# Attention with a gated unit on one core: a third bank shared by two engines, gates read from PSUM, and two small operations of the head moved

## The chip, the cores and the metric

The kernel runs on one core of a Trainium2 chip. The core has TensorE (PE; its weight loads are listed as PEld), VectorE (DVE), ScalarE (ACT), GpSimd (POOL) and SyncE (SP, which issues DMAs). The metric is the device time of one execution in microseconds; lower is better. Times of runs are given as medians, and one further execution was recorded by the hardware profiler.

## The reference

The input is 2048 rows of 640 numbers. Attention with 32 heads of 20 runs on the normalised rows, a gated unit with 1728 hidden columns runs on the same rows, and the two results are multiplied and added to the input:

```
xn = _layernorm(x, axis=-1)
q, k, v = split((xn @ wqkv), 32 heads of 20)
s = softmax(q k^T / sqrt(20)) v, heads joined, @ wo
h = sigmoid(xn @ w_gate) * (xn @ w_up)
g = silu(h @ w_down)
out = x + s * g
```

## The kernel before

**Head.** x is loaded in tiles of 128 rows. For each tile VectorE (two of the tiles: ScalarE) gathers mean and variance, ScalarE takes the root, VectorE inverts it and multiplies it with the negative mean (`ln_scale`, rstd L240, nb L241), GpSimd applies both (`ln_apply`, L245), TensorE transposes the tile (L254) and ScalarE copies it into xnT (L257). The first four heads of k are computed there; their largest absolute values (mk, L135 and L132) make a bound on the scores (`bound`, L318, ScalarE), TensorE adds it to q (L283), and ScalarE writes qT (L288). Behind its tiles GpSimd fills several buffers, the largest of them wo_pad (L357).

**Main part.** There are 32 passes, one for each quarter of the rows (512 queries) and each group of four heads. A pass has 64 banks: 16 tiles of 128 keys times four heads, each a score matmul of 512 columns into one PSUM bank (`score`, L1140). Most banks get their exp on ScalarE (`act_exp`, L1162): two sets of PSUM banks, sc0 with three and sc1 with two, are filled in turn, and one ACTIVATE does a whole set. Some banks get theirs on VectorE (`dve_exp`), in four instructions over 512 columns (dy L1173, du L1178, du L1182, p L1186); their scores go to a bank called spare, which is one of two banks (misc0, misc1) that all other matmuls use too. The probabilities are multiplied with v into a bank called oacc (`pv`, L1274), whose 21 rows for each head hold the sum of probabilities beside the result. When a pass is done, oacc is copied (L771), and the sums go through DRAM, are inverted and come back (L772 to L800).

**Between the exps** stand jobs that use TensorE's free time: gate and up products (L643, L656, with a tanh on ScalarE, L650, and a product on VectorE, L660), down products (`down_job`, L679: two halves of 320 columns, each copied to d2 by VectorE, L683; a tanh over 640 columns on ScalarE, L690; then a gate on VectorE, L695), output products (L718), and, for the last quarter, part products without the last two groups (`part_job`, L750, L755) to which GpSimd adds x by DMA (L758).

**The order is written out by a planner.** While the program is built, Python code keeps a clock for TensorE and a queue with durations and due times for ScalarE and VectorE, and emits the instructions in the order in which this plan starts them. Each engine then works its own list off in that order; what one needs of another is a semaphore wait. The planner lets TensorE multiply zeros into a free bank (`zero_add`, L1250) when fewer than 2.5 us of the last 3.4 us were counted as streaming. A cell (`Cell`) holds the planned time at which a bank or a value is free.

**The end.** The last pass is done in two halves of 256 queries. The first half's result is inverted in a job (`half_job`), the second half's behind the main loop (from L1369): copy of oacc, sums picked by a matmul (L1383), reciprocal (L1388), spread (L1390) and transposed by a matmul (L1392), scaled (L1394), multiplied with wo for the last two groups (L1376), gated (`gated`, L871), added up and sent out (`summed`, L874, L875).

Of the kernel before, what the change touches and what calls it, by code (L numbers as in the profile page):

```python
# [15 lines left out]
P = 128  # L16
HEAD = 32
GH = 4
# [26 lines left out]
def kernel(  # L45
# [116 lines left out]
    with tc.tile_pool(name="setup", bufs=1) as sp, \  # L162
# [76 lines left out]
        def ln_scale(t0, n):  # L239
            nc.vector.reciprocal(out=rstd[:, t0:t0 + n], in_=rstd[:, t0:t0 + n])  # L240
            nc.vector.scalar_tensor_tensor(out=nb[:, t0:t0 + n], in0=mv[:, t0:t0 + n, 0], scalar=-1.0,  # L241
                                           in1=rstd[:, t0:t0 + n], op0=ALU.mult, op1=ALU.mult)
# [68 lines left out]
        for c in range(4):  # L311
# [5 lines left out]
        op(("kbound",), "ACT", 0.3, [("kmost",)],  # L317
           lambda: nc.scalar.activation(out=bound, in_=esum, func=ACT.Identity, scale=mk[:, DENSE:DENSE + 1]))  # L318
# [56 lines left out]
    class Cell:  # L375
        def __init__(self, t=None):
            self.t = t

# [287 lines left out]
    def down_job(tt):  # L666
        c, t4 = divmod(tt, QC // P)
        yield "known", lambda: (bulk[0] == NFT and pe[0] > bulk_t[0] + LANDED and len(h_cells.get(c, [])) == NFT and (tt < 2 or tt - 2 in gq_cells)
                                and (c < NQC - 1 or front() >= PER_PASS * (NG * c + t4 + 1)))
        yield "wait", h_cells[c] + ([gq_cells[tt - 2]] if tt > 1 else [])  # L670
        hT = hTs[c]
        d2 = glu[0].tile([P, D], FP32, tag="d2", bufs=2, name="d2")
        got = []
        for h in range(2):
            e0_, e1_ = h * HALF, (h + 1) * HALF
            held, psd = yield "bank",
            for kf in range(NFT):
                fsz = fsz_list[kf]
                nc.tensor.matmul(psd[:, 0:HALF], lhsT=hT[0:fsz, kf, t4 * P:(t4 + 1) * P],  # L679
                                 rhs=glu[1][0:fsz, kf, e0_:e1_], start=(kf == 0), stop=(kf == NFT - 1))  # L680
                yield "mm", MM3
            got.append(dve.add(400.0, [Cell(pe[0] + PE_OUT)], lambda psd=psd, e0_=e0_, e1_=e1_:
                               nc.vector.tensor_copy(out=d2[:, e0_:e1_], in_=psd[:, 0:HALF]), 1))  # L683
            give_bank(held, got[-1])
        d_cells.setdefault(c, []).append(Cell(pe[0]))
        made = {}

        def tanh():
            made["t"] = glu[0].tile([P, D], BF16, tag="td", bufs=1, name="td")
            nc.scalar.activation(out=made["t"], in_=d2, func=ACT.Tanh, scale=0.25)  # L690

        def finish():
            last = c == NQC - 1
            gq = kT_all[:, t4, :].bitcast(FP32)[:, 0:D] if last else d2
            nc.vector.scalar_tensor_tensor(out=gq, in0=made["t"], scalar=1.0, in1=d2, op0=ALU.add, op1=ALU.mult)  # L695
            if last:
                gq_last[t4] = gq
            else:
                nc.gpsimd.dma_start(out=gq_dram[tt, :, :], in_=d2)

        turned = act.add(590.0, got + td_free[-1:], tanh, 0, EXP_LAG)
        td_free.append(dve.add(740.0, [turned], finish, 2))
        gq_cells[tt] = td_free[-1]
# [102 lines left out]
    half = {}  # L806

    def first_half(done):
        def copy():
            half["oev"] = glu[0].tile([P, KD, P], BF16, tag="wg", bufs=WB, name="oev")  # L810
            half["oev"] = half["oev"].rearrange("p k f -> p (k f)").bitcast(FP32)[:, 0:QH]
            nc.vector.tensor_copy(out=half["oev"], in_=oacc[:, 0:QH])

        cell = dve.add(340.0, [Cell(done + PE_OUT)], copy, -1)
        half["cell"] = cell
        return cell

    def half_job():
        n, tiles = QH // P, range(QH // P)
        yield "wait", [half["cell"]]  # L820
        held, pd = yield "bank",
        for t4 in tiles:
            nc.tensor.matmul(pd[:, t4 * GH:(t4 + 1) * GH], lhsT=half["oev"][:, t4 * P:(t4 + 1) * P], rhs=pick,
                             start=True, stop=True, skip_group_check=True)
            yield "mm", MM3
# [6 lines left out]
        def spread():  # L832
            made["rb"] = glu[0].tile([P, KD, P], BF16, tag="wu", bufs=WB, name="rb")
            made["rb"] = made["rb"].rearrange("p k f -> p (k f)").bitcast(FP32)[:, 0:n * P].rearrange(
                "p (t j i) -> p t j i", t=n, j=GH)
            nc.vector.tensor_copy(out=made["rb"], in_=made["rq"].unsqueeze(3).to_broadcast([P, n, GH, 32]))
# [6 lines left out]
        for t4 in tiles:  # L843
            nc.tensor.matmul(prl[:, t4 * P:(t4 + 1) * P], lhsT=made["rb"][:, t4, :, :].rearrange("p j i -> p (j i)"),
                             rhs=identf, start=True, stop=True, skip_group_check=True)
            yield "mm", 2 * MM5

        def scale():
            oTs[steps[-1]] = wk.tile([P, QC], BF16, tag="oT", bufs=NG + 3, name="oT")
            nc.vector.tensor_tensor(out=oTs[steps[-1]][:, 0:QH], in0=half["oev"], in1=prl[:, 0:QH], op=ALU.mult)  # L850

        cell = dve.add(340.0, [Cell(pe[0] + PE_OUT)], scale, -1)
# [4 lines left out]
        for t4 in tiles:  # L857
            got = []
            for h in range(2):
                held, ps = yield "bank",  # L860
                for g in range(NG - 2, NG):
                    nc.tensor.matmul(ps[:, 0:HALF], lhsT=oTs[NQC - 1, g][:, t4 * P:(t4 + 1) * P],
                                     rhs=wo_pad[:, g, h * HALF:(h + 1) * HALF], start=(g == NG - 2), stop=(g == NG - 1))
                    yield "mm", MM3
                got.append(dve.add(400.0, [Cell(pe[0] + PE_OUT)], lambda t4=t4, h=h, ps=ps: gated(t4, h, ps), 1))
                give_bank(held, got[-1])
            dve.add(740.0, [out_cells[(NQC - 1) * 4 + t4], *got], lambda t4=t4: summed(t4, pair[:, t4 % 2 * D:(t4 % 2 + 1) * D]), 2)
# [12 lines left out]
    LAST, QH = NB - PER_PASS, QC // 2  # L880
# [6 lines left out]
    HALF_COST = 12 * MM3 + 4 * MM5  # L887
# [46 lines left out]
    for t4 in range(4):  # L934
        jobs.append(Job(part_job(t4), PART_COST, len(steps) - 1, NB - (40 if t4 < 2 else 16)))
    jobs.append(Job(half_job(), HALF_COST, len(steps) - 1, NB - 12, when=lambda: half))
# [83 lines left out]
    def runnable(p):  # L1020
        k = 0
        while True:
            if k == len(flight):
                if k == MOST:
                    return None
# [12 lines left out]
    def fill(p, room=1e18):  # L1038
# [4 lines left out]
        pe_do("fill", took)  # L1043
# [24 lines left out]
    NEEDED, NEEDED_LAST = 6, 12  # L1068
# [36 lines left out]
    def dve_bank(banks):  # L1105
# [3 lines left out]
        ends = LAST + PER_PASS // 2 if LAST <= b < LAST + PER_PASS // 2 else PER_PASS * (b // PER_PASS + 1)  # L1109
# [12 lines left out]
    def unit(b):  # L1122
        return b // PER_PASS if b < LAST else len(steps) - 1 + (b - LAST) // (PER_PASS // 2)

    def pieces(b):
        r = b % PER_PASS
        if b < LAST:
            return [(r // GH, 0, 0, QC)]
        half, r = divmod(r, PER_PASS // 2)
        return [(2 * (r // GH) + k, half * QH, k * QH, QH) for k in range(2)]  # L1130

    def full(p):
        return KT if p < len(steps) - 1 else KT // 2
# [62 lines left out]
    def issue():  # L1196
# [6 lines left out]
        if (ci > 1 and dve.backlog + max(0.0, dve.t - pe[0]) < D_BACKLOG  # L1203
                and all(c.t is not None for c in d_made[-2:-1])):
            extra = dve_bank(taken)
            if extra is not None:
                split = take_bank("spare")
        ps = psum.tile([P, n, 512], FP32, tag=f"sc{ci % 2}", bufs=1, name="sc")
# [3 lines left out]
        sets[ci % 2] = act_exp(ps, taken, begun)  # L1212
# [10 lines left out]
    def pv_batch():  # L1223

        p = pv_pass[0]
        if p > len(steps):
            return None
# [36 lines left out]
    def pv(batch):  # L1264
# [3 lines left out]
        for k in range(2):  # L1268
            for part in range(1 if p < len(steps) - 1 else 2):
# [18 lines left out]
        if all(n == most for n in pv_count[0]):  # L1288
# [4 lines left out]
            elif p == len(steps) - 1:  # L1293
                oacc_free[0] = first_half(pe[0])
# [10 lines left out]
    while pv_pass[0] <= len(steps):  # L1305
# [47 lines left out]
        if zero_add(room):  # L1353
            idle = False
            continue
        soon = [q[k][1].made.t for q in ready_p for k in range(min(2, len(q)))]
        times = [until, pe[0] + 150.0] + [t + SEM for t in soon if t is not None]
        pe[0] = min(t for t in times if t > pe[0] + 1.0)

    while flight or jobs or timed or act.queue or dve.queue:  # L1360
# [5 lines left out]
    tiles = range(QH // P, QC // P)  # L1366
    units = [(t4, h) for t4 in tiles for h in range(2)]
    oev = wk.tile([P, QC], FP32, tag="oev", bufs=OBUFS, name="oev")
    nc.vector.tensor_copy(out=oev[:, QH:], in_=oacc[:, QH:])  # L1369
# [3 lines left out]
    banks, pd, prl = banks[1:5], banks[6], banks[7]  # L1373
# [6 lines left out]
    for bank, (t4, h) in zip(banks[:3], units):  # L1380
        out_mm(bank, t4, h, NG - 2)
    for k, t4 in enumerate(tiles):
        nc.tensor.matmul(pd[:, k * GH:(k + 1) * GH], lhsT=oev[:, t4 * P:(t4 + 1) * P], rhs=pick,  # L1383
                         start=True, stop=True, skip_group_check=True)
    out_mm(banks[3], *units[3], NG - 2)
# [5 lines left out]
    for k, t4 in enumerate(tiles):  # L1391
        nc.tensor.matmul(prl[:, t4 * P:(t4 + 1) * P], lhsT=rb[:, k, :, :].rearrange("p j i -> p (j i)"), rhs=identf,  # L1392
                         start=True, stop=True, skip_group_check=True)
    nc.vector.tensor_tensor(out=oTs[qc, g][:, QH:], in0=oev[:, QH:], in1=prl[:, QH:], op=ALU.mult)  # L1394
# [34 lines left out]
```

## Time and profile before

| | us |
|---|---|
| median of 3 runs | 894.62 (894.53 to 898.45) |
| the profiled execution | 898.68 |
| its span | 896.5 |
| ScalarE busy in the span | 871.4 (97%) |
| VectorE busy | 838.6 (94%) |
| TensorE busy | 809.1 (90%) |
| GpSimd busy | 161.6 (18%) |
| granted TensorE clock, mean | 0.99 |

The span is the time from the first to the last instruction of the profiled execution. An engine's busy time counts overlapping instructions once; the time of one instruction is longer than what it adds, because the next one starts before it has ended. Idle time is put down to whatever released the instruction behind it.

### The profile page before, as it was taken

Reading aid. Unit: us, or ns where it says so; the run is one execution under the profiler, and the core shown is the slowest. Engines: PE = TensorE matmul, PEld = TensorE weight load, DVE = VectorE, ACT = ScalarE, POOL = GpSimd, SP = SyncE. Lnnn points to the kernel's source line nnn. Section 1 sums busy time; section 2 is a strip of 40 time slices with the busy share of each in tenths; the row PEclk is TensorE's granted clock in tenths of the full one; section 3 lists DMA queues with packets and bytes.
Section 4 is the critical chain, followed back from the end, with each engine's and each line's share of the span. In section 5 each row is a group of like instructions: output and inputs, shape, how many; then the busy total and the mean of one; then the engine's idle time right before and its main releaser. Section 6 shows DMA issues by size and latency. Waiting matters only on the chain.

```text
span 896.5 us, 16915 instructions
## 1 busy us (share of the span) xinstructions
PE 809.1 (90%) x6228; PEld 291.8 (33%) x6311; DVE 838.6 (94%) x1483; ACT 871.4 (97%) x837; POOL 161.6 (18%) x305
## 2 busy tenths in 40 slices
PE   5899899998998999999999998999999888999896
PEld 3344333332223333232233332222332322333342
DVE  7799999999999999997999999999999989999994
ACT  6999999999999999999999999999999999999993
POOL 7401111101111212111111221110121220111120
PEclk9999999999999999999999999999999999999996
DMA  8113231235442234223212342303022432200021
GB/s 316 46 36 89 68 105 35 56 94 150 120 122 41 64 89 71 64 58 79 56 25 79 95 65 65 78 24 79 27 73 64 107 64 67 56 20 14 14 59 45
DMA packets 107672, 64.40 MB, mean 72 GB/s; under 512 B 80350, under 2 KB 101906, under 8 KB 107498
## 3 DMA queue, kind: packets, MB, share of 16 engines
q1 hardware_dynamic: 97382, 47.21, 19.8%
q0 software_dynamic: 10208, 16.11, 8.0%
q8 instruction: 49, 0.80, 0.4%
q14 instruction: 33, 0.27, 0.1%
HBM read 50.45 MB, written 16.13 MB: 74 GB/s over the span
## 4 chain that ended last, share of the span: by engine, by line
ACT 63%; issue 18%; PE 11%; DVE 7%; DMA 1%; SPq 0%; ACTq 0%; DVEq 0%
ACT p L1162 58%; PE sc L1140 4%; ACT tnh L650 3%; PE oacc L1274 2%; DVE dy L1173 1%; PE work L643 1%; PE work L123 1%; DVE du L1178 1%; PE work L679 1%; ACT td L690 1%; DVE stats L226 1%; DVE p L1186 1%; DVE du L1182 1%; PE work L149 1%; DMA x_sb<-in_A_x_dram 0%
## 5 line engine op out<-in xcount | busy, mean ns | idle before, releaser
L1162 ACT ACTIVATE p<-sc 128x1536 bf16<-128x1536 f32 x717 | 828.9, 1361 | 3.4 <-PE oacc L1274 1.4
L1140 PE MATMUL sc<-qT,kT_all 21*128 21x512 bf16 (+1 forms) x1850 | 280.9, 377 | 56.5 <-ACT p L1162 48.5
L1173 DVE TENSOR_SCALAR dy<-spare 128x512 f32<-128x512 f32 x256 | 175.2, 685 | 22.6 <-PE spare L1140 20.0
L1140 PEld LDWEIGHTS <-kT_all 21*128 21x128 bf16 x2112 | 90.9, 91 | 286.8 <-issue 275.1
L1182 DVE SCALAR_TENSOR_TENSOR du<-du,dy 128x512 f32<-128x512 f32 x256 | 174.1, 683 | 1.6
L1186 DVE SCALAR_TENSOR_TENSOR p<-du,dy 128x512 uint16<-128x512 f32 x256 | 174.0, 682 | 1.3
L1178 DVE SCALAR_TENSOR_TENSOR du<-dy 128x512 f32<-128x512 uint16 x256 | 174.2, 684 | 0.8
L1274 PE MATMUL oacc<-p,v_all 128*21 128x512 bf16 (+1 forms) x2112 | 158.3, 379 | 0.6 <-DVE v_all L156 0.3
L1140 PE MATMUL spare<-qT,kT_all 21*128 21x512 bf16 (+1 forms) x262 | 98.2, 379 | 0.0
L772 POOL DMA_DIRECT2D den_dram<-oev x31 | 17.9, 578 | 392.8 <-DVE oev L771 392.8
L679 PE MATMUL work<-wd,hT 128*128 128x320 bf16 x448 | 85.5, 302 | 0.1
L643 PE MATMUL work<-xnT,wg 128*128 128x512 bf16 (+1 forms) x261 | 77.6, 383 | 2.0 <-issue 0.6
L656 PE MATMUL work<-xnT,wu 128*128 128x512 bf16 (+1 forms) x268 | 73.1, 381 | 1.2 <-DVE dy L1173 0.3
L788 POOL DMA_DIRECT2D rl<-rec_dram x124 | 61.5, 502 | 57.6 <-DMA rec_dram<-den 47.8
L1250 PE MATMUL oacc<-xnT,zero 128*128 128x512 bf16 x169 | 57.9, 391 | 3.7 <-issue 2.9
L1274 PEld LDWEIGHTS <-v_all 128*21 128x21 bf16 x2112 | 31.4, 90 | 62.9 <-issue 60.7
L679 PEld LDWEIGHTS <-hT 128*128 128x128 bf16 x448 | 35.0, 97 | 48.7 <-issue 39.1
L650 ACT ACTIVATE tnh<-work 128x512 bf16<-128x512 f32 (+1 forms) x56 | 41.4, 738 | 0.0
L660 DVE SCALAR_TENSOR_TENSOR hT<-tnh,work 128x512 bf16<-128x512 bf16 (+1 forms) x56 | 38.0, 679 | 2.2 <-ACT tnh L650 1.9
L782 POOL DMA_DIRECT2D rec_dram<-den x31 | 16.9, 546 | 119.9 <-DVE den L781 115.4
L718 PE MATMUL work<-wo_pad,oT 128*128 128x320 bf16 x192 | 35.5, 302 | 0.5 <-issue 0.5
L643 PEld LDWEIGHTS <-wg 128*128 128x128 bf16 (+1 forms) x280 | 21.7, 98 | 42.8 <-issue 31.1
(122 smaller groups left out, 554.9 us busy)
## 6 DMA issues: line engine op xcount, KB each, us to landing
wg<-in_B_w_gate_dram SPq DMA_DIRECT2D x52, 160.0 KB
wu<-in_B_w_up_dram SPq DMA_DIRECT2D x52, 160.0 KB
rl<-rec_dram POOLq DMA_DIRECT2D x124, 64.0 KB, 2.4
qT<-q_dram SPq DMA_DIRECT2D x31, 128.0 KB
gq_dram<-d POOLq DMA_DIRECT2D x12, 320.0 KB, 2.5
gqr<-gq_dram SPq DMA_DIRECT2D x12, 320.0 KB
kT_all<-k_dram SPq DMA_DIRECT2D x28, 128.0 KB
wd<-in_B_w_down_dram SPq DMA_DIRECT2D x13, 160.0 KB
```

The costliest lines, as they stand in the source:

```text
L643: nc.tensor.matmul(psg[0:fsz, :], lhsT=wg[:, kd, 0:fsz], rhs=xnT[:, kd, cols], start=(kd == 0), stop=(kd == KD - 1))
L650: nc.scalar.activation(out=made["t"][0:fsz, :], in_=psg[0:fsz, :], func=ACT.Tanh, scale=0.5)
L656: nc.tensor.matmul(psu[0:fsz, :], lhsT=wu[:, kd, 0:fsz], rhs=xnT[:, kd, cols], start=(kd == 0), stop=(kd == KD - 1))
L679: nc.tensor.matmul(psd[:, 0:HALF], lhsT=hT[0:fsz, kf, t4 * P:(t4 + 1) * P], rhs=glu[1][0:fsz, kf, e0_:e1_], start=(kf == 0), stop=(kf == N ...
L788: nc.gpsimd.dma_start(out=t["rl"][32 * j:32 * j + 32, :], in_=rec_dram[n, j:j + 1, :].to_broadcast([32, QC]))
L1140: nc.tensor.matmul(ps[:, c0:c0 + n], lhsT=kT_all[rows, g, kt * P:(kt + 1) * P], rhs=qTs[qc, g][rows, q0:q0 + n], start=True, stop=True, ti ...
L1162: nc.scalar.activation(out=buf.tile(), in_=ps, func=ACT.Exp, bias=EXP_BIAS, scale=exp_scale)
L1173: nc.vector.tensor_scalar(out=t["y"], in0=ps, scalar1=LEAST, scalar2=None, op0=ALU.max)
L1178: nc.vector.scalar_tensor_tensor(out=t["u"], in0=t["f"], scalar=CUBE_2, in1=t["f"], op0=ALU.add, op1=ALU.mult)
L1182: nc.vector.scalar_tensor_tensor(out=t["u"], in0=t["u"], scalar=CUBE_1, in1=t["f"], op0=ALU.add, op1=ALU.mult)
L1186: nc.vector.scalar_tensor_tensor(out=buf.tile()[:, 0, :].bitcast(U16), in0=t["u"], scalar=CUBE_SCALE, in1=t["y"], op0=ALU.mult, op1=ALU.add)
L1274: nc.tensor.matmul(oacc[32 * j:32 * j + 1 + Dh, q0:q0 + width], lhsT=v_all[:, kt, GH * g + j, 0:1 + Dh], rhs=buf.ap[:, i, c0:c0 + width], ...
```

## The change

Four things are changed.

1. In the head, nb is made tile by tile with a `tensor_scalar`, rstd being a scalar operand, in place of one two-tensor operation for each batch; the first bound is made by VectorE in place of ScalarE.
2. A set of three banks may be shared: ScalarE gets two of them and VectorE the third, when no own bank is at hand and VectorE's planned backlog is under 1.3 us.
3. The halves of the down product are no longer copied: ScalarE's tanh and VectorE's gate read them in PSUM, 320 columns at a time.
4. The last pass is described by a list of parts (still 256 and 256 queries). Its jobs have other due times and other counted costs, are put first among the jobs in flight when their part is ready, and use other buffers. Zero matmuls stop ahead of the next planned probability, the sum of the first part's last tile is made behind the main loop, and four zero matmuls stand in the end.

The core of the diff:

```diff
+PARTS = ((0, 256), (256, 256))
...
-            nc.vector.scalar_tensor_tensor(out=nb[:, t0:t0 + n], in0=mv[:, t0:t0 + n, 0], scalar=-1.0,
-                                           in1=rstd[:, t0:t0 + n], op0=ALU.mult, op1=ALU.mult)
+            for t in range(t0, t0 + n):
+                nc.vector.tensor_scalar(out=nb[:, t:t + 1], in0=mv[:, t, 0:1], scalar1=rstd[:, t:t + 1], scalar2=-1.0,
+                                        op0=ALU.mult, op1=ALU.mult)
...
-        op(("kbound",), "ACT", 0.3, [("kmost",)],
-           lambda: nc.scalar.activation(out=bound, in_=esum, func=ACT.Identity, scale=mk[:, DENSE:DENSE + 1]))
+        op(("kbound",), "DVE", 0.15, [("kmost",)],
+           lambda: nc.vector.tensor_scalar(out=bound, in0=esum, scalar1=mk[:, DENSE:DENSE + 1], scalar2=None, op0=ALU.mult))
...
+        def tanh(h, psd):
+            made[h] = glu[0].tile([P, HALF], BF16, tag="td", bufs=2, name="td")
+            nc.scalar.activation(out=made[h], in_=psd[:, 0:HALF], func=ACT.Tanh, scale=0.25)
+        def gate(h, psd):
...
+            nc.vector.scalar_tensor_tensor(out=made["gq"][:, h * HALF:(h + 1) * HALF], in0=made[h], scalar=1.0,
+                                           in1=psd[:, 0:HALF], op0=ALU.add, op1=ALU.mult)
...
-            got.append(dve.add(400.0, [Cell(pe[0] + PE_OUT)], lambda psd=psd, e0_=e0_, e1_=e1_:
-                               nc.vector.tensor_copy(out=d2[:, e0_:e1_], in_=psd[:, 0:HALF]), 1))
-            give_bank(held, got[-1])
+            turned = act.add(320.0, [Cell(pe[0] + PE_OUT + 100.0), *td_free[-2:-1]], lambda h=h, psd=psd: tanh(h, psd), 0, EXP_LAG)
+            td_free.append(dve.add(400.0, [turned], lambda h=h, psd=psd: gate(h, psd), 1))
+            give_bank(held, td_free[-1])
...
-            yield "mm", MM3
+            yield "mm", 250.0, 0.0
...
-            yield "mm", 2 * MM5
+            yield "mm", 330.0, 200.0
...
+            end = lambda t4=t4: summed(t4, pair[:, t4 % 2 * D:(t4 % 2 + 1) * D])
+            if u == len(PARTS) - 2 and t4 == tiles[-1]:
+                later.append(end)
+            else:
+                dve.add(740.0, [out_cells[(NQC - 1) * 4 + t4], *got], end, 2)
...
+        shared = None
+        if (not split and n == 3 and ci > 1 and dve.backlog + max(0.0, dve.t - pe[0]) < SHARE
+                and all(c.t is not None for c in d_made[-2:-1]) and dve_bank(taken[:2]) == taken[2]):
+            shared = taken.pop()
         ps = psum.tile([P, n, 512], FP32, tag=f"sc{ci % 2}", bufs=1, name="sc")
         for i, b in enumerate(taken):
             score(ps[:, i, :], b)
             issued(b)
-        sets[ci % 2] = act_exp(ps, taken, begun)
+        sets[ci % 2] = act_exp(ps[:, 0:len(taken), :] if shared is not None else ps, taken, begun)
+        if shared is not None:
+            score(ps[:, 2, :], shared)
+            issued(shared)
+            sets[ci % 2] = Both(sets[ci % 2], dve_exp(ps[:, 2, :], shared, begun))
...
+        due = min([t for t in soon if t is not None], default=pe[0]) if b0 >= NB else 1e18
+        if zero_add(min(room, due - pe[0] - MM5)):
...
+    take_part(len(PARTS) - 1, pe[0])
     while flight or jobs or timed or act.queue or dve.queue:
...
-    for bank, (t4, h) in zip(banks[:3], units):
+    def keep_clock(n):
+        for _ in range(n):
+            nc.tensor.matmul(unused, lhsT=zero, rhs=xnT[:, 0, 0:512], start=True, stop=True, skip_group_check=True)
...
+    for end in later:
+        end()
...
+    keep_clock(2)
```

`Both` is a cell that is free when each of its two cells is. `first_half` and `half_job` are renamed to `take_part` and `last_job`, and take the part's number.

## The prediction

> **What bounds the kernel now.** I read four views in this order: the page's busy shares and chain, busy time by stretch, groups by form, and the timelines of head and end.
>
> ```profile
> PE 809.1 (90%) x6228; PEld 291.8 (33%) x6311; DVE 838.6 (94%) x1483; ACT 871.4 (97%) x837; POOL 161.6 (18%) x305
> ...
> ACT 63%; issue 18%; PE 11%; DVE 7%; DMA 1%; SPq 0%; ACTq 0%; DVEq 0%
> ```
>
> ScalarE is the fullest engine and carries most of the chain; VectorE is close behind. Busy time by stretch (columns: stretch, length, then PE, PEld, DVE, ACT, POOL busy; then TensorE clock):
>
> ```profile
> 60.00:860.00 800.00, 737.26 (x5585) 256.17 (x5662) 764.67 (x1312) 798.77 (x746) 128.47 (x236) 1.00 0.27 67
> 870.00:876.00 6.00, 5.63 (x76) 3.12 (x64) 5.32 (x13) 6.00 (x6) 2.93 (x5) 1.00 0.44 101
> 876.00:883.80 7.80, 7.47 (x66) 2.70 (x63) 3.98 (x7) 6.34 (x6) 0.00 (x0) 0.50 0.30 84
> 883.80:896.50 12.70, 5.35 (x36) 2.50 (x34) 4.68 (x10) 0.00 (x0) 0.00 (x0) 0.63 0.07 26
> ```
>
> Over 800 us ScalarE stands for 1.2 us, so there a us of ScalarE work, or of ScalarE waiting, is a us of kernel. At 876 the granted clock halves, and ScalarE loses time to TensorE for the first time. The last exp ends at 883.7; 12.8 us follow without ScalarE.
>
> The span is 896.53 us and this execution took 898.68, so 2.15 lie outside. The plain runs gave 894.53, 894.62 and 898.45. The profiled one is of the longer kind; the half-clock end (about 1.8 us of ScalarE gaps after 876, some 2 us more behind) is as large as that difference, so I read 894.6 as the same kernel with its clock kept. The sum goes against 898.68.
>
> **ScalarE's work.** From the timeline, start to start where the next instruction follows at once, medians: exp on 1536 columns 1330 ns, on 1024 columns 903.5, tanh on 512 (L650) 476.5, tanh on 640 from SBUF (L690) 627. The built order of the changed program has 341, 379 and 1 exps of three, two and one bank, where before had 358, 359 and 0: ten banks go to VectorE (266 for 256). The gain is 17 x 1.330 - 20 x 0.9035 - 0.48 = **4.1 us**. The sixteen 640-wide tanhs become 32 on 320 columns from PSUM. No such row exists. The PSUM rows lie on a line (50 ns + 0.833 ns a column), which gives 0.317; bounds are half the 640 row (0.31) and the whole 512 row (0.48). I take the line: 32 x 0.317 - 16 x 0.627 = **+0.1** (0 to +5). Four of the old tanhs started late, by 0.54, 0.48, 0.11 and 0.47 us, two of them behind this:
>
> ```profile
> L690 ACT ACTIVATE td<-d 128x640 bf16<-128x640 f32 x16 | 13.0, 812 | 0.6 <-ACT p L1162 0.3 <-DVE d L683 0.2
> L683 DVE COPY d<-work 128x320 f32<-128x320 f32 x32 | 15.3, 479 | 0.0
> ```
>
> The copies go; TensorE is late next. I take **-1.0** of 1.6 (0 to -1.6).
>
> VectorE loses 32 copies (0.40 each, start to start) and 16 gates of 640 (0.735), and gains 32 gates of 320 (0.40, as L724) and ten four-step exps (4 x 0.60): +12 us, inside the 35 us it idles between 60 and 860. That costs nothing while the cover lasts; without it, ScalarE would wait for late probabilities. Gating from PSUM holds a bank until both tanh and gate are done, which is why own-bank exps on VectorE fall from 256 to 247 in the built order, and 19 use the third bank of a shared set.
>
> **The shared sets add a wait.** The third bank is a slice of the tile that ScalarE reads, and the built order shows that two readers of one tile are put one behind the other:
>
> ```
> Activation p2_3803<-sc_3785 128x1024 [waits DVE_49,Activation_49]
> TensorScalarPtr dy_3071<-sc_3055 128x512 [waits Activation_49]
> ```
>
> In before no exp waits for VectorE and no dy for ScalarE. Now ten exps wait for dy on the same set (case A), and nine dys for the exp (case B).
>
> A: scores end a median 0.29 us ahead of their exp in the trace; dy starts 0.07 or more behind its score and takes 0.68 (L1173); a semaphore takes about 0.07. ScalarE, its queue blocked, waits 0.07 + 0.68 + 0.07 - 0.29 = 0.53: ten make 5.3. Between the tenth and the eightieth percentile of that lead (0.10 to 0.58) it is 0.24 to 0.72.
>
> B: an exp of two banks lasts 1.14 from start to end; then 0.07, dy 0.68, 0.07, and the next scores 0.40: 2.36 after the exp began the set is full again. ScalarE has the other set until 1.81. It waits 0.55, less where a tanh (0.48) stands between; 0.45 x 9 = 4.1. From below 0 (a tanh each time), from above 0.9. Behind the waiting dy stand the other exps and gates of VectorE, which its idle time takes up. Together **+9.4** (2 to 15).
>
> **The head.** nb becomes a TENSOR_SCALAR for each tile (16 for 12), and the first bound moves from ScalarE (L318, 0.39 us) to VectorE. Timelines of POOL, DVE and ACT:
>
> ```profile
> 20.71 2.59 POOL L245 TENSOR_SCALAR x_sb<-x_sb,rstd,nb 128x640 bf16<-128x640 bf16 x3 [0.52 <-DVE nb L241]
> 27.99 4.69 POOL L357 MEMSET wo_pad<- 128x5120 bf16 x1
> ```
>
> ```profile
> 20.95 0.64 DVE L241 SCALAR_TENSOR_TENSOR nb<-mv,rstd 128x1 f32<-128x1 f32 x1
> ...
> 28.40 0.16 DVE L132 TENSOR_REDUCE mk<-mk_all 128x1 f32<-128x4 f32 x1
> ```
>
> ```profile
> 28.90 0.39 ACT L318 ACTIVATE bound<-esum,mk 128x128 bf16<-128x128 bf16 x1
> 29.77 0.69 ACT L288 ACTIVATE qT<-ps_q,e_one 128x512 bf16<-128x512 f32 x1 [0.48 <-PE ps_q L283]
> ```
>
> The nb at 20.95 takes 0.64 where others take 0.16: it ends at 21.59, as the first of POOL's three instructions ends (20.71 + 0.86). So a VectorE instruction can wait out a whole POOL instruction; another lost 0.43 at 8.93. The reduction at 28.40 ran at its usual 0.16 beside a POOL memset, so not each one does. Which kind is the new bound? It reads and writes 16-bit data in SBUF, like L568, which does 512 columns in 0.29 us where other forms take 0.68: it uses more access to SBUF than a plain stream, as the two-input nb does. So L241 is the row it is nearest to. It would be ready at 28.56, in the middle of the 4.69 us memset, and wait until 32.68. From bound's start to the first exp before took 30.99 - 28.90 = 2.1; less 0.2 for the shorter instruction, the exp starts at 34.6: **+3.6**. If it does not wait, bound ends near 28.8, qT follows the two kT_all at about 29.3, and the head gains 0.5. nb by itself: two stalls of 0.45 gone at best, 16 at 0.14 (L522) for 12 at 0.11 at worst (+0.9); taken as 0. POOL's order is unchanged.
>
> The Trainium skill, page "SBUF — State Buffer", section "Who interferes with whom", says that a copy, cast or tensor_scalar in a mode using two ports, and a GpSimd instruction, exclude each other for the whole instruction of whichever starts first. It speaks against this edit; the stalls of L241 agree, while no row here shows a TENSOR_SCALAR of VectorE beside a POOL memset. By it the first exp is at 34.6, without it at 30.5.
>
> **The end.** The rest of the last pass is counted by what it streams, with filler matmuls only up to the next probability, so I expect the clock to hold: -1.8 us of ScalarE gaps. Before, the last PV batch waited behind six zero matmuls at half clock and ended at 886.23, 2.5 us behind the last exp; now 0.45. But the built order puts work behind it that had been done earlier: one part product, the gating and sum of tile 1, and VectorE's sum of tile 0. Two gates 0.8, the part product 0.85 and its gate 0.4, the sum 0.74 and the waits between set the reciprocal about 4.0 behind the last exp, as before (4.05). The stretch behind it (8.7) stays. End: **-2.0** (-4 to +1).
>
> **Sum.** -4.1 + 0.1 - 1.0 + 9.4 + 3.6 - 2.0 = +6.0: 898.7 + 6.0 = **904.7**, 10 above the median shown.
>
> **Rivals.**
> - Bound isn't held (the reduction at 28.40 speaks for it): 904.7 - 4.1 = 900.6.
> - Not slower: the waits of shared sets are covered, because dy runs ahead of need. It decides on dy ending before ScalarE is through the other set, so a lead of 0.82 us or more, against the median 0.29. Sum without 9.4, and no hold: 898.7 - 7.5 = 891.2; with the hold 895.3.
> - Worse: with TensorE idle for 4 us in the head its clock drops as at 876, and dys stand behind other work: 4 more, 908 to 909.
> - Not doing what it says: the clock halves in the end all the same: +2 to +4 on any of these.
>
> Chances: forecast 0.5, not held 0.27, covered 0.15, worse 0.08. The range 896 to 909 holds the first two with their bounds and some of the others. A measurement can tell about 0.5% here (890.1 to 899.1 is no change): faster 0.05, same 0.19, slower 0.76.
>
> **What would show it.** An exp p2<-sc waiting for DVE dy, about ten times 0.5 us; ScalarE gaps after dy on sc; ACT exp busy 4 us less; bound on VectorE lasting 4 us, ending with wo_pad's memset, first exp near 34.6; clock 1.00 past 876; reciprocal some 4 us behind the last exp. I am wrong if ScalarE's idle time between 60 and 860 stays at 1 to 2 us, or bound takes 0.2.

## The result, and the profile after

The changed kernel takes **916.37 us** (913.97 to 918.28, 4 runs), the kernel before 896.46 us beside it: a ratio of 1.0229, 95% interval 1.0205 to 1.0252. The four runs of before are two near 894.6 and two near 898.4. The forecast was 904.7, the range ended at 909: the direction held, the size did not. The profiled execution of the changed kernel took 918.11 (span 916.2), 19.4 more than the profiled one of before.

Busy shares, chain and the exps' group on the page after:

```profile
PE 812.6 (89%) x6212; PEld 292.5 (32%) x6294; DVE 855.3 (93%) x1512; ACT 871.2 (95%) x856; POOL 161.6 (18%) x305
...
ACT 50%; PE 17%; issue 16%; DVE 15%; POOL 1%; DMA 1%; SPq 0%; DVEq 0%; ACTq 0%; POOLq 0%
...
L1185 ACT ACTIVATE p<-sc 128x1536 bf16<-128x1536 f32 (+2 forms) x721 | 829.1, 1319 | 17.3 <-PE sc L1163 9.4
```

ScalarE is busy as long as before (871.2 to 871.4) in a span 19.7 longer, though its exps are fewer: where nothing follows at once, an instruction counts with its full length (1.58 us for an exp of 1536 columns, against 1.33 from start to start). VectorE's share of the chain has doubled from 7 to 15%: it now stands between exps. Three places hold the time: from the span's start to the first exp 35.57 us (30.99 before), from there to the end of the last exp 865.0 (852.7; below, this is the stretch of exps), behind it 15.6 (12.8).

**The head.** Timelines of POOL, DVE, ACT and PE, after:

```profile
28.05 4.69 POOL L359 MEMSET wo_pad<- 128x5120 bf16 x1
...
28.51 4.42 DVE L320 TENSOR_SCALAR bound<-esum,mk 128x128 bf16<-128x128 bf16 x1
...
33.40 1.54 PE L150 MATMUL ps_v<-wv,xnT 128*128 128x160 bf16 x10 [5.22 <-DVE v_all L157]
...
33.70 0.69 ACT L290 ACTIVATE qT<-ps_q,e_one 128x512 bf16<-128x512 f32 x1 [4.28 <-remote]
```

Bound starts 0.46 us after the memset and ends at 32.93, 0.19 after it. qT waits for it, and TensorE is idle for 5 us; its clock halves at 30.72, 2.5 us after its last matmul ended (28.17).

**The shared sets.** Waits after (columns: total, times, longest); none of the three is in the trace of before:

```profile
DVE dy L1196 <- ACT p L1185: 9.5, 9, 1.4
...
PE sc L1163 <- DVE dy L1196: 7.3, 9, 1.3
...
ACT p L1185 <- DVE dy L1196: 4.3, 8, 1.6
```

One set of each kind in the timeline. First dy behind its exp, then an exp behind its dy:

```profile
215.54 0.69 DVE L1196 TENSOR_SCALAR dy<-sc 128x512 f32<-128x512 f32 x1 [1.18 <-ACT p L1185]
...
216.29 0.39 PE L1163 MATMUL sc<-qT,kT_all 21*128 21x512 bf16 x3 [1.20 <-DVE dy L1196]
...
216.72 1.45 ACT L1185 ACTIVATE p<-sc 128x1536 bf16<-128x1536 f32 x1 [0.30 <-PE spare L1163]
...
267.96 0.68 DVE L1196 TENSOR_SCALAR dy<-sc 128x512 f32<-128x512 f32 x1
...
268.74 3.28 ACT L1185 ACTIVATE p<-sc 128x1024 bf16<-128x1024 f32 x3 [0.50 <-DVE dy L1196]
```

From dy's start to ScalarE's next start it takes 1.18 us in the first case (0.69 of dy, the hand-over, the scores) and 0.78 in the second (dy and the hand-over).

**The clock.** Busy time by stretch (columns as in the prediction):

```profile
30.72:37.55 6.83, 4.15 (x19) 2.27 (x20) 3.36 (x6) 2.14 (x2) 2.87 (x8) 0.50 0.08 16
37.55:218.46 180.91, 167.45 (x1307) 63.96 (x1319) 175.40 (x317) 177.98 (x158) 22.21 (x42) 1.00 0.27 74
218.46:221.87 3.41, 3.08 (x15) 0.51 (x14) 3.41 (x7) 2.96 (x3) 0.00 (x0) 0.50 0.07 14
...
269.66:279.90 10.24, 9.87 (x35) 2.29 (x35) 6.50 (x11) 6.96 (x8) 0.00 (x0) 0.50 0.21 49
279.90:727.04 447.14, 405.89 (x3081) 141.97 (x3122) 427.18 (x730) 443.00 (x431) 76.91 (x140) 1.00 0.27 64
727.04:730.45 3.41, 3.41 (x20) 1.01 (x17) 3.41 (x7) 1.93 (x2) 1.08 (x2) 0.50 0.47 79
```

TensorE's granted clock halves three times in the middle (and in the head from 30.72 to 37.55). In the middle TensorE is then the full engine, and from 269.66 on ScalarE works 6.96 of 10.24 us. Past 876, where the profile before fell to half, the clock is 1.00 up to 911.36.

**The end.** Timeline after, then the instructions of the closing line (columns: shortest, median, longest in ns; first and last start) of after and of before:

```profile
904.35 0.87 POOL L767 DMA_DIRECT2D hT<-in_A_x_dram  x1 [7.90 <-DVE hT L764]
...
905.10 0.21 DVE L1428 RECIPROCAL rq<-last 128x8 f32<-128x8 f32 x1 [0.32 <-PE last L1420]
...
909.85 0.83 DVE L890 TENSOR_TENSOR ot<-kT_all,hT 128x640 bf16<-128x640 f32 x1
```
```profile
L1465 POOLq DRAIN  x3: 51/93/11086, 904.3 to 915.9; - x3
L1465 SPq DRAIN  x3: 7/7/7, 913.0 to 915.7; - x3
```
```profile
L1424 POOLq DRAIN  x3: 51/102/11127, 874.3 to 896.2; - x3
L1424 SPq DRAIN  x3: 7/7/7, 895.7 to 896.0; - x3
```

POOL's closing drain lasts 11.1 us in both, from its last DMA on. Before, it was over at 885.4. After, that DMA (x added to the last tile's part product) is issued at 904.35, behind the last exp, and the drain ends at 915.4: SyncE, done at 913.0, waits for it.

### The profile page after: what moved, and what is told of

The parts are those of the page before. It is cut to its first block, busy times and chain, and to the rows that moved or that the text cites. A ratio compares the mean times of both kernels' runs of the same rounds, so it can differ in the third digit from the quotient of the medians.

```text
span 916.2 us, 16861 instructions
## 1 busy us (share of the span) xinstructions
PE 812.6 (89%) x6212; PEld 292.5 (32%) x6294; DVE 855.3 (93%) x1512; ACT 871.2 (95%) x856; POOL 161.6 (18%) x305
## 3 DMA queue, kind: packets, MB, share of 16 engines
q1 hardware_dynamic: 97382, 47.21, 19.4%
## 4 chain that ended last, share of the span: by engine, by line
ACT 50%; PE 17%; issue 16%; DVE 15%; POOL 1%; DMA 1%; SPq 0%; DVEq 0%; ACTq 0%; POOLq 0%
ACT p L1185 46%; PE sc L1163 5%; DVE dy L1196 4%; DVE du L1201 3%; PE oacc L1305 2%; DVE du L1205 2%; PE work L666 2%; PE work L653 2%; DVE p L1209 2%; ACT tnh L660 2%; PE work L705 1%; PE work L124 1%; ACT td L687 1%; DVE stats L227 1%; PE work L586 1%
## 5 line engine op out<-in xcount | busy, mean ns | idle before, releaser
L1185 ACT ACTIVATE p<-sc 128x1536 bf16<-128x1536 f32 (+2 forms) x721 | 829.1, 1319 | 17.3 <-PE sc L1163 9.4
L1205 DVE SCALAR_TENSOR_TENSOR du<-du,dy 128x512 f32<-128x512 f32 x266 | 180.3, 682 | 1.9
L1196 DVE TENSOR_SCALAR dy<-spare 128x512 f32<-128x512 f32 x247 | 168.3, 683 | 14.7 <-PE spare L1163 13.4
L1209 DVE SCALAR_TENSOR_TENSOR p<-du,dy 128x512 uint16<-128x512 f32 x266 | 180.3, 681 | 1.6
L1201 DVE SCALAR_TENSOR_TENSOR du<-dy 128x512 f32<-128x512 uint16 x266 | 180.3, 682 | 1.0
L1163 PE MATMUL spare<-qT,kT_all 21*128 21x512 bf16 (+1 forms) x255 | 94.9, 377 | 0.0
L1281 PE MATMUL oacc<-xnT,zero 128*128 128x512 bf16 x153 | 51.5, 385 | 2.6 <-issue 1.9
L660 ACT ACTIVATE tnh<-work 128x512 bf16<-128x512 f32 (+1 forms) x56 | 38.0, 679 | 0.1
L666 PEld LDWEIGHTS <-wu 128*128 128x128 bf16 (+1 forms) x280 | 24.1, 99 | 40.8 <-issue 24.7
```

The source lines that it names most:

```text
L660: nc.scalar.activation(out=made["t"][0:fsz, :], in_=psg[0:fsz, :], func=ACT.Tanh, scale=0.5)
L666: nc.tensor.matmul(psu[0:fsz, :], lhsT=wu[:, kd, 0:fsz], rhs=xnT[:, kd, cols], start=(kd == 0), stop=(kd == KD - 1))
L1163: nc.tensor.matmul(ps[:, c0:c0 + n], lhsT=kT_all[rows, g, kt * P:(kt + 1) * P], rhs=qTs[qc, g][rows, q0:q0 + n], start=True, stop=True, ti ...
L1185: nc.scalar.activation(out=buf.tile(), in_=ps, func=ACT.Exp, bias=EXP_BIAS, scale=exp_scale)
L1196: nc.vector.tensor_scalar(out=t["y"], in0=ps, scalar1=LEAST, scalar2=None, op0=ALU.max)
L1201: nc.vector.scalar_tensor_tensor(out=t["u"], in0=t["f"], scalar=CUBE_2, in1=t["f"], op0=ALU.add, op1=ALU.mult)
```

## The experiments

**One or three parts undone.** e1:

```diff
-        op(("kbound",), "DVE", 0.15, [("kmost",)],
-           lambda: nc.vector.tensor_scalar(out=bound, in0=esum, scalar1=mk[:, DENSE:DENSE + 1], scalar2=None, op0=ALU.mult))
+        op(("kbound",), "ACT", 0.3, [("kmost",)],
+           lambda: nc.scalar.activation(out=bound, in_=esum, func=ACT.Identity, scale=mk[:, DENSE:DENSE + 1]))
```

> The changed kernel with one line undone: the first bound is an ACTIVATE of ScalarE again, nb and all else as changed. Theory (VectorE's bound is held behind POOL's 4.69 us memset of wo_pad): bound lasts 0.39 us, the first exp starts 4.1 to 4.6 us earlier (near 31), and the time falls by as much, to about 912 from 916.4. Rival (the head is late because the v matmuls stand ahead of the first scores on TensorE, and the clock falls there): bound is short, but the first exp moves by 1 us or less. A second rival: the head is early again but the planner's order behind it is set, so ScalarE waits later instead and the time falls by less than half of it.

Measured: 908.66 (906.77 to 915.07, 6 runs), 7.7 less. The first exp is at 30.98, the clock stays 1.00 from 16 to 879.7 in the profile, and the stretch of exps takes 858.9. The 7.7 are more than the 4.1 to 4.6 of the theory: in this profile the half clock of the head is gone, and so are the drops in the middle. The six runs differ by the clock, from 906.77 at a mean of 0.995 to 915.07 at 0.984.

e2:

```diff
-    NEEDED, NEEDED_LAST, SHARE = 6, 12, 1300.0
+    NEEDED, NEEDED_LAST, SHARE = 6, 12, -1.0
```

> The changed kernel with the threshold for sharing set to -1.0, so that no set is shared: 358 and 359 exps of three and two banks as before the change, gates from PSUM, the last pass and the head as changed. Theory (exp and dy on one set wait for each other, about 10 us, and the stalls of TensorE behind them bring the clock down for some 7 us more): from first exp to last exp's end 849 to 851 us instead of 865.0 (852.7 before the change, less 1.8 for the cold end and 1 to 1.6 for late tanhs), clock 1.00 in all of the middle, and the time falls by 14 to 16 us to about 901. Rival (the loss is VectorE's fullness: gates from PSUM hold banks and dys come late): ScalarE's gaps stay, the time falls by 5 us or less. Between: waits yes, clock drops not theirs: 8 to 9 us.

Measured: 904.28 (899.80 to 905.78, 6 runs), 12.1 less; the stretch of exps is 854.0, 3 us above the 851 expected at most, and these lie at its start, at half clock from 32.70 to 42.94. From 42.94 to 896.27 the clock is 1.00. VectorE's fullness as the cause falls.

e3:

```diff
-        for x in [x for x in jobs if x.when is not None and x.when()]:
-            jobs.remove(x)
-            flight.insert(sum(y.when is not None for y in flight), x)
```

> The changed kernel with one piece undone: the job of the last pass's first half is no longer put ahead of the jobs in flight as soon as its sums are taken, so the part products of the last four tiles, with POOL's adding DMAs, come before it as before the change. Theory (POOL's closing drain lasts 11.1 us behind its last DMA in both profiles, 874.31 to 885.44 before the change and 904.33 to 915.41 after; only after it does it end later than the output's DMA): POOL's last DMA is issued 5 us or more ahead of 904.35, the drain is covered, and from the last sum on VectorE to the end of the span it takes 3.1 to 3.2 us instead of 5.5: the time falls by about 2.4 us. Less work stands behind the last exp as well: up to 1.5 us more. Rival (the output's own DMAs set the end): 0, or some tenths from the shorter work.

Measured: 915.12 (913.67 to 918.47, 4 runs). The closing line of e3:

```profile
L1462 POOLq DRAIN  x3: 51/98/11087, 899.6 to 916.2; - x3
L1462 SPq DRAIN  x3: 7/7/7, 915.6 to 915.9; - x3
```

POOL's last DMA moves to 899.66, its drain ends at 910.7, and from VectorE's last sum (913.31) to the end of the span it takes 3.14 instead of 5.52: the drain no longer counts, as expected. The total falls by 1.25 only, less than the runs of either kernel lie apart, so the saving does not show in the time: 11.6 us lie between last exp and last sum, 10.1 in the changed kernel, and the mean clock in between is 0.64 here, 1.00 there.

e4 holds these three edits together.

> The changed kernel with the three edits of the other runs of this call undone together (bound on ScalarE, no shared sets, the last job not put ahead): what is left is the gates from PSUM, nb one tile at a time, and the last pass counted and filled as changed. Theory: the parts add up, 4.4 + 15 + 2.4 = 22 less than the changed kernel, 893 to 896; against the kernel before the change (896.5) 0 to 3.5 us faster. Rival (gates from PSUM or the last pass cost something by themselves): over 899. Rival (the parts overlap, since an early head is waited away later): 897 to 903.

Measured: 896.10 (895.34 to 898.82, 12 runs), ratio to before 1.0019 (1.0008 to 1.0029). So bound, sharing and the order of the last job hold the loss but for 1.3 us.

**What holds bound.** e12 is e2 with one line more:

```diff
+        nc.gpsimd.tensor_copy(out=wo_pad[:, 0, 0:1], in_=bound[:, 0:1])
         nc.gpsimd.memset(wo_pad.rearrange("p g d -> p (g d)"), 0.0)
```

> The kernel of e2_no_share (no shared sets; bound on VectorE, where it lasted 4.43 us beside POOL's memset of wo_pad; 904.28 us) with one instruction more: ahead of that memset POOL copies one column of bound, so the memset, whole as before, starts only when bound is written. Theory (POOL's running memset is what holds bound): bound lasts 0.25 us or less right after the reduction before it, first exp at 29.7 to 30.4, clock 1.00 in the head, time 894 to 896, as e10_two (895.16), which has bound on ScalarE. Rival (bound on VectorE is slow by itself): bound lasts 4 us though POOL does nothing, the memset comes after 33, and nothing is gained.

Measured: 894.34 (893.67 to 898.20, 12 runs), ratio to before 0.9996 (0.9983 to 1.0010). Timelines of DVE, POOL and ACT of e12:

```profile
28.75 0.25 DVE L320 TENSOR_SCALAR bound<-esum,mk 128x128 bf16<-128x128 bf16 x1
...
29.31 4.36 POOL L360 MEMSET wo_pad<- 128x5120 bf16 x1
...
29.55 0.69 ACT L290 ACTIVATE qT<-ps_q,e_one 128x512 bf16<-128x512 f32 x1
```

The same instruction takes 0.25 us when POOL doesn't run beside it: the 4.42 were the memset.

e5 is e4 with bound on VectorE and the memset cut:

```diff
-        nc.gpsimd.memset(wo_pad.rearrange("p g d -> p (g d)"), 0.0)
+        for g in range(NG):
+            nc.gpsimd.memset(wo_pad[:, g, :], 0.0)
```

> The kernel of e4_three (no shared sets, last job not put ahead; 896.1 us, first exp at 30.05) with the bound on VectorE again, and POOL's memset of wo_pad cut in eight, one for each group of heads (0.6 us each instead of 4.69 once). Theory (VectorE's bound is held for as long as the one POOL instruction that it meets): bound lasts 0.9 us or less, the first exp starts at 29.7 to 30.6, the clock keeps 1.00 in the head, and the time is 895 to 897. Rival (bound on VectorE is late or slow by itself, or the v matmuls take its place): first exp at 34 or later, as in e2_no_share (35.58), and 900 or more. Second rival (POOL's pieces follow so closely that VectorE never gets between them): bound lasts 4 us as before the cut.

Measured: 905.17 (904.90 to 907.69, 4 runs); the second rival. POOL and DVE of e5:

```profile
28.23 4.98 POOL L360 MEMSET wo_pad<- 128x640 bf16 x8
...
28.68 4.73 DVE L320 TENSOR_SCALAR bound<-esum,mk 128x128 bf16<-128x128 bf16 x1
```

VectorE got in between none of the eight pieces. The first exp starts at 36.05, and the clock is half from 32.08 to 45.73.

e13 is e2 with TensorE kept busy:

```diff
         def q_bound():
+            for _ in range(20):
+                nc.tensor.matmul(first["ps"], lhsT=zero, rhs=xnT[:, 0, 0:QC], start=False, stop=False, skip_group_check=True)
```

> The kernel of e2_no_share (bound held, first exp at 35.58, TensorE at half clock from 32.70 to 42.94, 904.28 us) with twenty matmuls of zeros, 512 columns each, added into ps_q ahead of the bound's own matmul: TensorE streams for some 4.3 of the 5 us in which it had nothing to do. Theory (the head loses twice: 5 us of waiting, and some 4 us more because TensorE, idle for 5 us, is then granted half its clock): bound and the first exp are as late as before (35 to 36), but the clock keeps 1.00 and ScalarE's gaps in the first 50 us fall back from over 4 to about 2 us: time 899.5 to 901. Rival (the 4 us come from the late start itself, or the clock falls whatever TensorE does): time within 1 us of 904.3, half clock as before.

Measured: 898.80 (898.47 to 900.12, 5 runs). The same stretch of e2 and of e13, busy time and clock:

```profile
28.00:43.00 15.00, 10.17 (x38) 3.77 (x35) 9.20 (x13) 7.04 (x9) 5.59 (x9) 0.66 0.07 16
```
```profile
28.00:43.00 15.00, 14.20 (x89) 6.09 (x87) 12.56 (x19) 10.39 (x12) 5.86 (x9) 1.00 0.08 20
```

Bound lasts 4.43 in both, and the first exp of e13 still starts at 34.98; but with the clock at 1.00 instead of 0.66 ScalarE works 10.39 of these 15 us instead of 7.04, and 5.5 us of the median are gone. In medians the head thus cost 3.6 by waiting (898.80 less the 895.16 of e10, below) and 5.5 by the clock. The two profiled executions differ by 2.6 only; the runs of e2 go from 899.80 at a mean clock of 0.996 to 905.78 at 0.985, and where the clock was low in those that were not profiled isn't known. The Trainium skill, page "TensorE: Matmul & The Clock Gate", section "What's actually happening", says that TensorE falls to half its clock after an idle window of about 3.4 us. e2 agrees (4.83 us idle, half clock 4.5 us after the last matmul); in the changed kernel the clock fell after 2.5 us. The drops in the middle of the changed kernel don't: TensorE was busy for 59 to 69% of the 3.41 us ahead of each.

**The shared sets by themselves.** e11 is e4 with SHARE at 1300.0 again, e1 with the last job not put ahead.

> The kernel of e1_bound_act (shared sets, bound on ScalarE, 908.66 us) with the last pass's first half not put ahead; or e4_three (896.1 us) with the 19 shared sets made again. Theory of the shared sets: from first exp to last exp's end 858 to 859 as in e1_bound_act (e4_three 850.9). Theory of the end: POOL's last DMA comes ahead of the last exp's end, the drain is covered, and 12 to 13 us lie behind the last exp instead of 15.64. Time 903 to 905. Rival (shared sets delay the part products by themselves, whatever the order of jobs): POOL's last DMA still 2 us or more behind the last exp, 15 us behind it, 906 to 908.

Measured: 905.07 (903.82 to 905.98, 4 runs): 9.0 above e4. The stretch of exps is 860.1, with two stretches of half clock (800.86 to 804.27, 879.36 to 882.78); 13.1 us lie behind it, and POOL's last DMA (888.58) is ahead of the last exp's end (890.83). With the last job ahead (e1) 15.64 lie behind it, and the drain sets the end.

e6 is e4 with SHARE at 2600.0.

> The kernel of e4_three (no shared set, 896.1 us, from first exp to last exp's end 850.9) with sharing at a threshold of 2600 instead of none: 39 shared sets (20 with the exp behind dy, 19 the other way round) and 325 and 402 exps of three and two banks instead of 358 and 359. Theory (each shared set costs ScalarE some 0.53 us): 39 x 0.53 = 20.7 of waits less 33 x 1.330 - 43 x 0.9035 = 5.0 of exps: the stretch grows by some 16 us to 866 with the clock kept, and by what clock drops add; the time is 911 to 920, the more so than e1_bound_act, where 19 sets made the stretch 858.9. Rival (the loss came from a few unlucky places, not from each set): stretch 856 to 861, time 901 to 906.

Measured: 918.30 (918.11 to 922.82, 5 runs), stretch 873.1, at clock 1.00 from 19 to 913: 22.2 more than e4 with 5.0 us less work, so 27 us of waits in 39 sets, 0.70 each, or 0.63 without an early one, at 40.8, that costs 3.1. Each set costs, as the theory has it, and on average more than in e1 (0.50, below).

e9 is e4 with SHARE at 1300.0 and the order told to the planner (`exp_done` is a new argument of `dve_exp`, the planned end of the exp on the same set):

```diff
-        first = dve.add(606.0, [Cell(begun + MM5 + PE_OUT - 100.0), *d_made[-2:-1]], bits, 0, 114.0)
+        first = dve.add(606.0, [Cell(begun + MM5 + PE_OUT - 100.0), exp_done, *d_made[-2:-1]], bits, 0, 114.0)
...
-            sets[ci % 2] = Both(sets[ci % 2], dve_exp(ps[:, 2, :], shared, begun))
+            sets[ci % 2] = Both(sets[ci % 2], dve_exp(ps[:, 2, :], shared, begun, sets[ci % 2]))
```

> The kernel of e4_three with sharing at the changed kernel's threshold of 1300, and the planner told of the order: dy of a shared set is planned behind the exp of that set, so that all 20 shared sets have dy behind exp, and TensorE's next scores, PV and filler matmuls are planned around it. 341 and 381 exps of three and two banks: 2.7 us less work for ScalarE. Theory (the wait is in the set itself: ScalarE has two sets, and one is blocked for an exp and a dy one after the other): ScalarE still loses about 0.5 us at most of the 20, stretch 856 to 860; but TensorE is given other work meanwhile, so the clock drops less often; time 901 to 905. Rival (the waits come only from the planner's ignorance): ScalarE's gaps return to those of e4_three, stretch 848 to 850, time 893 to 895.

Measured: 901.18 (900.93 to 902.26, 6 runs), stretch 857.5. The stretch from 60 to 860 of e10 (no shared sets), e1 (19) and e9 (20, planned):

```profile
60.00:860.00 800.00, 735.85 (x5582) 256.27 (x5659) 754.53 (x1292) 799.41 (x763) 129.31 (x236) 1.00 0.27 67
```
```profile
60.00:860.00 800.00, 744.06 (x5577) 254.26 (x5573) 767.27 (x1319) 791.29 (x759) 128.11 (x234) 1.00 0.27 67
```
```profile
60.00:860.00 800.00, 736.63 (x5528) 255.59 (x5608) 763.50 (x1310) 792.23 (x762) 128.25 (x234) 1.00 0.27 67
```

ScalarE stands for 0.6, 8.7 and 7.8 us. Planning gives TensorE other work, and the clock reads 0.998 in all six runs, but ScalarE waits nearly as much as before: the wait is in the set.

**What is left.** e10 is the changed kernel with bound on ScalarE and no sharing.

> The changed kernel with bound on ScalarE and no shared sets, but with the last pass's first half put ahead of the jobs in flight, as changed: e4_three with that one piece made again. In e2_no_share, which has it too, 11.1 us lay behind the last exp, and POOL's drain ended 0.4 us ahead of VectorE's last instruction; in e4_three 12.66. Theory (without the shared sets' delays POOL's last DMA is early enough, and the order then saves what stood behind the last exp): 1 to 1.5 us less than e4_three, 894.3 to 895, about the kernel before. Rival (the drain sets the end here too): 0 to 2 us more than e4_three.

Measured: 895.16 (894.36 to 901.06, 12 runs), ratio to before 1.0014 (0.9996 to 1.0032); 11.1 us behind the last exp, POOL's drain over at 889.1 of 893.2. The early job by itself is harmless: it takes the shared sets' delay for the drain to set the end. Five of the twelve runs read a mean clock of 0.986 to 0.992 and take 897.6 to 901.1, so the clock can fall without a held bound and without shared sets.

e8 is the kernel before with gates from PSUM and nb tile by tile, as in the change.

> The kernel before the change with two parts of it alone: gates and tanhs of the down projection straight from PSUM, and nb one tile at a time. Neither shared sets, nor bound on VectorE, nor the last pass counted anew. Theory (32 tanhs of 0.317 for 16 of 0.627 cost 0.1, and the late tanhs, 0.5 to 1.6 us, go): 893.5 to 894.7, 0.1 to 1.2 us faster than before. Rival (a bank held until tanh and gate are both done delays scores or dys): 895.5 to 898.

Measured: 899.08 (899.01 to 899.38, 5 runs), ratio to before 1.0042 (1.0030 to 1.0054): slower. In the middle nothing is lost (ScalarE works 799.54 of 800 us from 60 to 860). But 12.0 us lie between last exp and last sum (9.7 in the profile before): the planner now puts all gates of the first half behind the last exp. The time lies above the theory and above the rival; these 2.3 us are part of the 3.9 lost (899.08 against 895.17), and where the rest lies is open. With the last pass recounted as well the loss is smaller (e4 1.3 us, e10 0.3).

## Why the prediction was too low

The profiled execution took 13.4 us more than the forecast of 904.7: 1.0 in the head, 9.7 in the stretch of exps (12.3 longer than before, 2.6 by the prediction's terms) and 3.0 behind it (2.8 longer, 0.2 shorter by the prediction), and 0.24 less outside the span.

In medians the change comes apart so: e10 against before +0.3 (895.16 and 894.81); bound on VectorE +9.1 (e2); sharing on top of both +12.1. The parts depend on the order: with sharing in place, bound counts 7.7 (e1). The prediction had +3.6 for the head and 9.4 - 4.1 = +5.3 for sharing.

- **ScalarE's work: right.** 341, 379 and 1 exps, tanhs 0.317 us apart as taken from the line through the PSUM rows. The late tanhs brought some 0.3 instead of 1.0. This is read from ScalarE's excess, the time by which its starts lie further apart than the medians of the prediction: from first exp to 850 it is 13.1 us in before and 12.8 in e8.
- **Shared sets' waits: right, a little low.** In e1, where the clock holds in the middle, ScalarE lost 0.48 us at each of the ten exps behind dy and 0.53 at each of the nine dys behind an exp: 9.6 for 9.4 predicted, and about 1 more one start later. The rival "covered" fell: the lead of 0.29 us decided, as the prediction said.
- **Bound: right.** 4.42 us, ending with the memset; the first exp 4.6 later instead of 3.6, since TensorE did the v matmuls of the head at half clock ahead of the first scores (2.8 us from the memset's end to the first exp, in e13 at full clock 2.0). The one-tile nb no longer waits (0.21 each). e12 shows the cause. The Trainium skill, page "SBUF — State Buffer", section "Who interferes with whom", has a tensor_scalar of VectorE in a mode using two ports and a GpSimd instruction exclude each other for the whole instruction; e12 and e2 agree (0.25 and 4.43), and e5 adds that eight pieces one after the other held as one. The row the prediction leaned on, the two-input nb, is another kind: a one-column nb is a TENSOR_SCALAR too, and it did not wait beside POOL.
- **The failed step: the clock.** The sum held the clock at 1.00 everywhere but in the last 40 us. "TensorE idle for 4 us in the head" was left to a rival with a chance of 0.08 and 4 us, though the forecast itself produced that idle time, and the fall at 876 was on the page. The rival likened the two; at 876 TensorE was not idle but busy for 89% of the 3.41 us before. The half clock came true in every profile with bound held (after, e2, e3, e5) except e13, where TensorE was kept streaming. In the profile after, half clock cost 0.9 us ahead of the first exp, about 1.2 behind it (ScalarE's excess in the first 100 us: 4.1, before 2.9) and some 6.6 in the middle (excess of ScalarE in the same shared sets: 8.6 us between 200 and 300 after, 3.8 in e1; 6.0 and 4.3 between 700 and 800). These are 8.7 of the 13.4 us; without them the profiled execution would stand at 909.4, still past the range, and the end accounts for that.
- **The end: half right.** The clock stayed up, and the reciprocal stood 4.5 behind the last exp (4.0 predicted). But "the stretch behind it (8.7) stays" failed: it took 11.1, since POOL's last DMA had moved behind the last exp, and the drain of 11.1 us behind it, which before was hidden, set the end. The prediction counted that part product and its gate, not the DMA it issues. The drain makes 2.4 of the 3.0 us (5.52 from the last sum to the end of the span, 3.14 in e3).
- **The base.** The forecast stood against the profiled 898.68, and counted 2.0 for a clock that is kept at the end. Of 17 runs of the kernel before, beside e10, 15 take 894.6 to 895.2 at a mean clock of 0.996 to 0.998, and two 898.4 and 899.1 at 0.991: the clock was mostly kept already.

**Open:** what starts a drop of the clock in the middle. I held that the stalls behind shared sets bring the drops. All three in the middle of the changed kernel come within 3 us of a dy on a shared set (215.54, 267.96 and 726.07), and one of e11 too, but not the one of e3 (536.28), and e6 speaks against a simple rule: twice the sets, and in its profile no drop in the middle, though TensorE was busy for as little as 55% of some 3.41 us there. (Two of its five runs read 0.990 and take 922.7 to 922.8.) In e9, where the least is 67%, no run dropped.

The traces narrow it down. Within one execution, all starts of half clock, and all ends ahead of the closing one, lie whole multiples of 3.413 us apart, so each profile can be cut into windows on that grid. Count each matmul by the share of the 128x128 array that it fills (a score with its 21 rows, or a PV with its 21 columns, fills a sixth; 512 columns last 0.216 us, the shortest usual distance of zero matmuls): the windows ahead of the 28 drops in the 14 profiles then hold 0.32 or less (the six between 60 and 870: 0.28 to 0.32), where the median window holds 0.54, and of the 3533 other windows at full clock from 20 us on 17 are as low. Busy time does not separate them: 0.89 ahead of the fall at 876, and 0.57 in a window of the changed kernel (from 901.1) behind which the clock held. So it may be that a TensorE busy with matmuls that fill little of the array loses its clock much as an idle one does. This was read off the traces afterwards; no run was made to test it.

Also not tried is a shared set whose two readers, which read different banks of it, are not put in order.

## What to carry to other kernels

Before work goes to the engine with idle time, look at what runs beside it there and what the builder makes wait: an operation of 0.25 us took 4.4 beside a long GpSimd instruction, and a bank given to a second engine blocked its whole set for both. Where a prediction makes TensorE idle for some microseconds, price the half clock behind it as part of the forecast. And follow each moved step to its last DMA: a queue that needs 11 us to close is free only while something else ends later.

## What the runs showed of the hardware

- Eight GpSimd memsets, one right after another and 4.98 us together, held a VectorE TENSOR_SCALAR for 4.73 us; one memset of 4.69 us held it for 4.42.
- POOL's closing drain took 11.09 to 11.13 us from its last DMA on in all 14 profiles, whenever that was.
- Stretches of half clock that ended before the closing one lasted 3.41, 6.83, 10.24 or 13.65 us: one to four times 3.41. Within one execution, their starts and ends lie on one grid of 3.413 us.
